# An earlier release of a conversion's exponent tile, and GpSimd subtractions made in two halves, in a fused attention and gated-layer kernel

## The chip, the cores and the metric

The kernel runs on one core of one Trainium2 chip. A core has TensorE (matrix products; in the rows PE, its weight loads PEld), VectorE (DVE), ScalarE (ACT), GpSimd (POOL) and SyncE (SP, which here issues most DMAs). Each works through its own list of instructions in order and waits on semaphores for the others. The metric is the device time of one execution in microseconds; lower is better.

## The reference

Two layers, one behind the other, in float32. The first is an attention in which a query sees only the keys of its own hash bucket (4 batches, 8 heads, 768 positions, 64 columns a head); the second is a gated layer on 3072 rows of 512 columns, with 1536 columns between.

```python
q_bits = np.einsum('bhsd,dk->bhsk', q, proj) > 0      # 6 sign bits, k likewise
mask = q_bucket[:, :, :, None] == k_bucket[:, :, None, :]
scores = np.where(mask, q @ k.T / 8, -1e9)
attn = softmax(scores) @ v                             # 4 x 8 x 768 x 64
x = attn as 3072 x 512
gate = 1 / (1 + np.exp(-(x @ w_gate)))                 # weights are float64
out = (gate * (x @ w_val)) @ w_out
```

The three weights of the gated layer arrive as float64 and the chip's engines calculate in float32.

## The kernel before, in words

**Two stages.** Stage 1 is the attention, with the first two products of the gated layer at its end, and beside it the conversion of most weights. Stage 2, from 428.7 us of the span, is the gated layer: TensorE goes through products `z` (L1178) and `y` (L932) with weights that GpSimd's queue fetches back (L1728).

**The attention.** Work goes in pairs of heads (16 pairs, named batch_pair, as 3_1), each in two groups of three tiles of 128 query rows. For a tile and head, a *score task* of TensorE (8 matmuls, `sc`, L1551 and L1557) fills one of three PSUM places called `two`; VectorE takes the least value and moves the tile to SBUF (`e<-sc`, L1569), which frees the place; ScalarE forms the exponentials (L1578). When the six exponentials of a group are there, six *turns* (12 transposes each, `tp<-ident,e`, L1614) go through the same three places `two`; each is copied back by ScalarE or VectorE (`e<-tp`, L1620). Then come six *value tasks* (`pv`, L1630), which add up in another place of PSUM, and the division `xs` (L1637).

Ahead of a pair, its k and q are turned (`tk`, `tq`, L1358), copied (`rawk`, `rawq`), rounded to a high part (`kh`, `qh`, ScalarE or GpSimd), and the low part is the rest, `kl = rawk - kh` (L1389, GpSimd or VectorE, 768 columns). The parts of q are also sent through DMAs to swapped halves (`qsl`, `qsh`, L1418). The *hash* of a pair (`h`, L1452) gives sign bits on VectorE (`kq<-h`, L1458), which are sent to DRAM (`bd<-kq`, L1461) and back in another layout (`kq<-bd`, L1468 and L1470); the first score task of the pair needs them.

**A weight conversion** (`floats`, L674) makes float32 out of 512 columns of float64. VectorE picks the exponent bits (`exponent`, L689, tile `ex`), ScalarE shifts them (L692), VectorE picks the mantissa (`mantissa`, L697, tile `mf`), adds the low word (L702) and puts the sign in `ex` (L707); GpSimd multiplies `mf` by `ex` (`scaled`, L712). In `load_pair` (L802) four sums (L821 to L824) make seven blocks out of four, and the result is split in a high part (L830) and a low part (L833, 896 columns), which are sent to DRAM (L836) for stage 2. 34 conversions stand in stage 1: 20 for the pairs, and 10 of `w_out` and 4 for the early products, which have no sums and are split in L766 and L769. 6 more stand in stage 2, where VectorE and ScalarE do GpSimd's part.

**What sets the order.** A planner (`Plan.order`) goes through a model of the engines and writes each engine's instructions in the order in which they start in it. Every task names what it needs (`after`), which counted places it takes and gives back (`take`, `give`), and a key. TensorE's order is a written table, `ORDER`; the other engines take the ready task with the smallest key, and the table `SHIFT` moves keys. `stock` holds the number of places; `mid1=1` is the one place that a conversion of stage 1 takes ahead of its exponent and gives back after its low part. Since the conversions' tasks are numbered in both tables, each new task gives new tables.

Of the kernel before, what the change touches and what calls it, by code (L numbers as in the profile page):

```python
# [111 lines left out]
]  # L112
SHIFT = {
# [394 lines left out]
def lsh_attention_glu_kernel(ctx, tc, q, k, v, proj, w_gate, w_val, w_out, out):  # L508
# [132 lines left out]
    def busy():  # L641
        nc.tensor.matmul(idle, zero[:, :P], zero, start=True, stop=True)  # L642

    W_KEY, W_STEP, W_MORE = 2.0, 1.5, 0.2
    stock = dict(
        one=2, two=3, moe=1, y=0, kr=1, qr=1, vr=2, h=2, e=3, st=3, su=3, sv=2, rb=2, xs=3,
        raw1=1, mid1=1, raw2=2, mid2=1, wk=1, xr=1, x2=1, x3=1, ob=3,
        t=0, zt=0, ws0=0, ws1=0, ws2=0, xb=0, r0=0, r1=0, r2=0, x1=0, x4=0, x5=0, x6=0, wk2=0,
    )
    WS = 3  # L650
# [1126 lines left out]
```

## Time and profile before

| | |
|---|---|
| median of 3 runs | 964.09 us (963.86 to 966.96) |
| the profiled execution's own time | 965.6 us |
| its span | 963.8 us |
| TensorE busy | 952.0 us (99%) |
| VectorE, ScalarE, GpSimd busy | 608.2, 548.2, 274.3 us |
| stage 1 (to 428.7 us) / stage 2 | 428.7 us / 535.1 us of the span |

The span is the time from the first to the last instruction in the profile; 1.8 us of the execution's own time lie around it. "Busy" of TensorE counts a matmul from its start to a modelled end, so small waits between matmuls hide in it; starts of one kind of task, one behind the other, show them better.

### The profile page before, as it was taken

Reading aid. Unit: us, or ns where it says so; the run is one execution under the profiler, and the core shown is the slowest. Engines: PE = TensorE matmul, PEld = TensorE weight load, DVE = VectorE, ACT = ScalarE, POOL = GpSimd, SP = SyncE. Lnnn points to the kernel's source line nnn. Section 1 sums busy time; section 2 is a strip of 40 time slices with the busy share of each in tenths; the row PEclk is TensorE's granted clock in tenths of the full one; section 3 lists DMA queues with packets and bytes.
Section 4 is the critical chain, followed back from the end, with each engine's and each line's share of the span. In section 5 each row is a group of like instructions: output and inputs, shape, how many; then the busy total and the mean of one; then the engine's idle time right before and its main releaser. Section 6 shows DMA issues by size and latency. Waiting matters only on the chain.

```text
span 963.8 us, 20105 instructions
## 1 busy us (share of the span) xinstructions
PE 952.0 (99%) x8067; PEld 774.8 (80%) x8070; DVE 608.2 (63%) x1173; ACT 548.2 (57%) x993; POOL 274.3 (28%) x325
## 2 busy tenths in 40 slices
PE   9999999999999999999999999999999999999998
PEld 5666665666666567689999999999999999999997
DVE  7999898999899898676656743334633336333332
ACT  5988898898888889554334433324433235333322
POOL 4444655666765665630000000000000000000000
PEclk9999999999999999999999999999999999999999
DMA  7666888888897877489966774444744444644421
GB/s 186 175 194 189 224 252 241 244 249 238 263 268 213 233 228 228 171 315 411 370 237 230 280 262 175 153 153 154 271 170 158 170 177 173 222 154 153 154 78 66
DMA packets 116606, 204.37 MB, mean 212 GB/s; under 512 B 63456, under 2 KB 87968, under 8 KB 110624
## 3 DMA queue, kind: packets, MB, share of 16 engines
q1 hardware_dynamic: 107456, 118.08, 39.9%
q0 software_dynamic: 6688, 84.42, 23.7%
q8 instruction: 63, 1.03, 0.4%
q10 hardware_dynamic: 2368, 0.59, 0.3%
q14 instruction: 31, 0.25, 0.1%
HBM read 147.84 MB, written 43.42 MB: 198 GB/s over the span
## 4 chain that ended last, share of the span: by engine, by line
PE 92%; DVE 4%; DMA 2%; ACT 1%; issue 1%; SPq 0%; ACTq 0%; DVEq 0%
PE y L932 20%; PE pv L1630 12%; PE zBg L1178 10%; PE zBv L1178 10%; PE sc L1557 9%; PE tp L1614 7%; PE zDv L1178 5%; PE zDg L1178 5%; PE sc L1551 4%; PE zAg L1178 2%; PE zAv L1178 2%; PE h L1452 1%; DVE e L1569 1%; PE zg L896 1%; PE zv L896 1%; PE idle L642 1%
## 5 line engine op out<-in xcount | busy, mean ns | idle before, releaser
L1569 DVE TENSOR_SCALAR_CACHE_REDUCE e<-sc 128x768 f32<-128x768 f32 x192 | 177.1, 952 | 20.3 <-PE sc L1557 18.5
L1578 ACT ACTIVATE e<-e,st 128x768 f32<-128x768 f32 x192 | 178.9, 933 | 15.1 <-DVE e L1569 13.2
L932 PE MATMUL y<-wo,gh 128*128 128x512 f32 x480 | 151.0, 396 | 0.0
L1630 PE MATMUL pv<-e,vr 128*64 128x384 f32 x768 | 140.7, 496 | 0.0
L1620 ACT COPY e<-tp 128x768 f32<-128x768 f32 x144 | 112.2, 795 | 27.9 <-PE tp L1614 27.1
L1614 PEld LDWEIGHTS tp<-ident,e 64*128 64x128 f32 x2304 | 87.0, 138 | 45.7 <-issue 13.7
L1178 PE MATMUL zBg<-x,wsg 128*128 128x384 f32 x552 | 111.0, 335 | 0.0
L1178 PE MATMUL zBv<-x,wsv 128*128 128x384 f32 x552 | 110.7, 335 | 0.0
L1178 PEld LDWEIGHTS zBg<-x,wsg 128*128 128x128 f32 x552 | 98.2, 188 | 6.6 <-ACT t1g L1186 0.4
L1178 PEld LDWEIGHTS zBv<-x,wsv 128*128 128x128 f32 x552 | 98.3, 188 | 6.0
L932 PEld LDWEIGHTS y<-wo,gh 128*128 128x128 f32 x480 | 89.9, 187 | 15.2
L1614 PE MATMUL tp<-ident,e 64*128 64x64 f32 x2304 | 99.6, 226 | 1.8 <-DVE e L1569 0.9
L1271 ACT CAST gh<-zt 128x384 fp32r<-128x384 f32 x92 | 47.1, 514 | 95.1 <-DVE zt L1266 75.5
L932 PE MATMUL y<-wo,gl 128*128 128x512 f32 x240 | 93.2, 388 | 0.0
L1557 PE MATMUL sc<-kh,ql 64*128 64x384 f32 x192 | 89.8, 468 | 0.0
L1557 PE MATMUL sc<-kh,qsl 64*128 64x384 f32 x192 | 89.8, 468 | 0.0
L1630 PEld LDWEIGHTS pv<-e,vr 128*64 128x64 f32 x768 | 48.2, 136 | 51.3 <-issue 43.0
L1728 POOL DMA_DIRECT2D wsv<-kzv x23 | 12.2, 532 | 236.9 <-PE zDg L1178 224.6
L1728 POOL DMA_DIRECT2D wsg<-kzg x23 | 12.3, 536 | 227.4 <-PE zDv L1178 206.9
L1250 ACT ACTIVATE sig<-sig 128x384 f32<-128x384 f32 x69 | 36.2, 525 | 61.7 <-DVE sig L1193 61.6
L1274 DVE TENSOR_TENSOR gl<-zt,gh 128x384 fp32r<-128x384 f32 x92 | 51.0, 554 | 29.2 <-ACT gh L1271 29.2
L1551 PE MATMUL sc<-kq 64*128 64x384 bf16 x384 | 64.8, 328 | 2.3 <-ACT e L1620 1.1
(214 smaller groups left out, 1964.4 us busy)
## 6 DMA issues: line engine op xcount, KB each, us to landing
wsg<-kzg POOLq DMA_DIRECT2D x23, 1792.0 KB, 8.1
wsv<-kzv POOLq DMA_DIRECT2D x23, 1792.0 KB, 7.6
kzg<-wkg SPq DMA_DIRECT2D x12, 896.0 KB
kzv<-wkv SPq DMA_DIRECT2D x12, 896.0 KB
rawg<-in_moe_w_gate_dram SPq DMA_DIRECT2D x14, 512.0 KB
rawv<-in_moe_w_val_dram SPq DMA_DIRECT2D x14, 512.0 KB
vr<-in_v_dram SPq DMA_DIRECT2D x16, 384.0 KB
rb<-rd SPq DMA_DIRECT2D x64, 96.0 KB
```

Source lines behind the costliest of these rows:

```text
L932: nc.tensor.matmul(acc, a[:, slot, ts_], w, start=(first and i == 0), stop=(last and i == 2), skip_group_check=cols != slice(None),)
L1178: nc.tensor.matmul(acc, streams[n, jp][:, c, wa, a_], X[x_][:, xa, c], start=first and c == 0 and i == 0, stop=c == 1 and i == 2, skip_gro ...
L1250: lambda blk=blk: nc.scalar.activation(sig[:, blk], w["B"][:, :GN] if blk == 2 else sig[:, blk], AF.Sigmoid),
L1271: nc.scalar.copy(side["h"][:, blk], w["z", blk])
L1274: eng.tensor_sub(side["l"][:, blk], w["z", blk], f(side["h"][:, blk]))
L1551: nc.tensor.matmul(sc[:, j, :GN], kq[z["h"]][rows, 2 + 2 * g + h, t * P : (t + 1) * P], kq[z["h"]][rows, h], start=True, stop=False, tile_ ...
L1557: nc.tensor.matmul(sc[:, j, :GN], q_[rows, c], z["k" + x][rows, h * GN : (h + 1) * GN], start=False, stop=(m == 2), tile_position=(j * D, 0),)
L1569: nc.vector.tensor_scalar(sp(e), gz["sc", t, h][:, :, :GN], -MASKED * SCALE, None, op0=ALU.min, op1=ALU.min, accum_out=gz["st", t][:, h : ...
L1578: nc.scalar.activation(e, e, AF.Exp, bias=st[:, h : h + 1], scale=-1.0, accum_out=gz["su"][:, h * GT + t : h * GT + t + 1],)
L1614: nc.tensor.transpose(tp[:, r, at_ : at_ + D], gz["e", t, h][rows, c * P : (c + 1) * P], ident[rows, rows], tile_position=(r * D, 0),)
L1620: copy(gz["e"][:, :, c * P : (c + 1) * P].rearrange("p n (r d) -> p r n d", r=2), gz["tp", c][:, :, :GN].rearrange("p r (n d) -> p r n d", ...
L1630: nc.tensor.matmul(gz["pv"][rows, :GN], z["v"][:, h, c], gz["e"][:, h * GT : (h + 1) * GT, c * P : (c + 1) * P], start=(c == 0), stop=(c = ...
```

## The change

The exponent tile has a place of its own, `ex1`, taken by `exponent` and given back when GpSimd's `scaled` is done with it; `mid1` is now taken by `mantissa`. The low part of a converted pair in stage 1 is made in two pieces of 512 and 384 columns, and the low parts of k and q in two pieces of 384, and each piece may go to GpSimd or VectorE. Both tables of the order are new throughout.

```diff
     stock = dict(
-        raw1=1, mid1=1, raw2=2, mid2=1, wk=1, xr=1, x2=1, x3=1, ob=3,
+        raw1=1, mid1=1, ex1=1, raw2=2, mid2=1, ex2=1, wk=1, xr=1, x2=1, x3=1, ob=3,
...
-        b1 = add(key, "dve", 336, exponent, after=[a], take=["mid" + own], port=0.92)
+        b1 = add(key, "dve", 336, exponent, after=[a], take=["ex" + own], port=0.92)
         b2 = add(key, "act", 628, shifted, after=[b1])
-        c1 = add(key, "dve", 400, mantissa, after=[b1], port=0.92)
+        c1 = add(key, "dve", 400, mantissa, after=[b1], take=["mid" + own], port=0.92)
...
-            key, "dve" if last else "pool", 680 if last else 1240, lambda: scaled(nc.vector if last else nc.gpsimd), after=[d], port=0.92
+            key, "dve" if last else "pool", 680 if last else 1240, lambda: scaled(nc.vector if last else nc.gpsimd), after=[d], give=["ex" + own], port=0.92
...
-        def low(eng):
-            eng.tensor_sub(y["w"][:, 1], y["f"], f(y["w"])[:, 0])
+        def low(eng, c=slice(None)):
+            eng.tensor_sub(y["w"][:, 1, c], y["f"][:, c], f(y["w"])[:, 0, c])
...
-        m = add(key, [("dve", 1005, lambda: low(nc.vector))] if last else
-                [("pool", 2078, lambda: low(nc.gpsimd)), ("dve", 1005, lambda: low(nc.vector))], after=[h], give=["mid" + own], port=0.92)
+        m = h
+        for cut, n_ in ((slice(0, 4), 4), (slice(4, SL), SL - 4)) if not last else ((slice(None), SL),):
+            m = add(key, [("dve", 1005, lambda: low(nc.vector))] if last else
+                    [("pool", 180 + 280 * n_, lambda cut=cut: low(nc.gpsimd, cut)), ("dve", 70 + 134 * n_, lambda cut=cut: low(nc.vector, cut))],
+                    after=[h, m], give=["mid" + own] if last or n_ < 4 else [], port=0.92)
...
-                eng.tensor_sub(z[n + "l"], z["raw", n], f(z[n + "h"]))
+                c = slice(half * GN, (half + 1) * GN)
+                eng.tensor_sub(z[n + "l"][:, c], z["raw", n][:, c], f(z[n + "h"][:, c]))
...
-                needs.append(add(
-                    n_, [("pool", 1930, lambda n=n: part(n, "l", nc.gpsimd)), ("dve", 870, lambda n=n: part(n, "l", nc.vector))],
-                    after=[a], port=0.92,
-                ))
+                b_ = None
+                for half in range(2):
+                    b_ = add(
+                        n_, [("pool", 1030, lambda n=n, half=half: part(n, "l", nc.gpsimd, half)),
+                             ("dve", 470, lambda n=n, half=half: part(n, "l", nc.vector, half))],
+                        after=[a, b_], port=0.92,
+                    )
+                needs.append(b_)
```

What the new order does to the lists of instructions is shown at three places. First GpSimd where pair 2_3's k and q are split (`kl`, `ql`) beside a conversion's split (`wk`). Before:

```order
L1389 TENSOR_TENSOR kl2_3_4831<-rawk2_3_4797,kh2_3_4830 128x768
L830 CAST wkg31_4883<-mfg3_1_4735 128x896
L833 TENSOR_TENSOR wkg31_4883<-mfg3_1_4735,wkg31_4883 128x896
L1389 TENSOR_TENSOR ql2_3_4897<-rawq2_3_4871,qh2_3_4896 128x768
L1585 TENSOR_SCALAR su2_148<-su2_148 128x6
```

And now:

```order
L1422 TENSOR_TENSOR kl2_3_4862<-rawk2_3_4822,kh2_3_4861 128x384
L859 CAST wkv31_4890<-mfv3_1_4749 128x896
L862 TENSOR_TENSOR wkv31_4890<-mfv3_1_4749,wkv31_4890 128x512
L862 TENSOR_TENSOR wkv31_4890<-mfv3_1_4749,wkv31_4890 128x384
L1422 TENSOR_TENSOR ql2_3_4959<-rawq2_3_4929,qh2_3_4958 128x384 x2
```

Each subtraction stands as two; the other half of `kl` has moved to VectorE. Over the whole kernel GpSimd's 25 subtractions of 768 columns become 45 of 384, and VectorE's 5 become 15; of the 20 of 896 columns, 35 pieces stay on GpSimd and 5 go to VectorE.

Second VectorE, around one conversion (`exo`, `mfo`) between the least values of score tasks (`e<-sc`). Before:

```order
L1569 TENSOR_SCALAR e2_1_0_4315,st2_1_0_0_4314<-sc2_1_0_0_1_4317 128x768
L689 TENSOR_SCALAR exo5_4369<-rawo5_4184 128x512
L1620 COPY e2_0_1_4084<-tp2_0_1_0_4336 128x2x6x64
L697 TENSOR_SCALAR mfo5_4380<-rawo5_4184 128x512
L702 SCALAR_TENSOR_TENSOR mfo5_4380<-rawo5_4184,mfo5_4380 128x512
L707 SCALAR_TENSOR_TENSOR exo5_4369<-rawo5_4184,exo5_4369 128x512
```

And now, at a conversion close by:

```order
L718 TENSOR_SCALAR exo4_4112<-rawo4_3981 128x512
L1606 TENSOR_SCALAR e2_0_1_4100,st2_0_1_0_4099<-sc2_0_1_0_1_4090 128x768
L1606 TENSOR_SCALAR e2_0_1_4100,st2_0_1_1_4138<-sc2_0_1_1_0_4103 128x768
L726 TENSOR_SCALAR mfo4_4145<-rawo4_3981 128x512
L1626 RECIPROCAL su1_147<-su1_147 128x6
L1628 STREAM_TRANSPOSE sv2_0_0_4150<-su1_147 128x32
L731 SCALAR_TENSOR_TENSOR mfo4_4145<-rawo4_3981,mfo4_4145 128x512
L736 SCALAR_TENSOR_TENSOR exo4_4112<-rawo4_3981,exo4_4112 128x512
```

The exponent now stands two least values ahead of the mantissa here; over the 34 conversions of stage 1 it stands 1 to 4 places ahead in both orders.

Third TensorE at the end of the scores of pair 1_1, where the turns of its first group begin. Before:

```order
L1557 MATMUL sc1_1_1_2_1_2829<-kh1_1_2062,qh1_1_2117 128x384
L1614 MATMUL tp1_1_0_2_2841<-ident_170,e1_1_0_2505 128x64 x12
L1630 MATMUL pv1_1_0_2855<-e1_1_0_2505,vr1_1_2458 64x384 x2
L1630 MATMUL pv1_0_1_2564<-e1_0_1_2237,vr1_0_1950 64x384 x2
L1630 MATMUL pv1_1_0_2855<-e1_1_0_2505,vr1_1_2458 64x384 x2
L1630 MATMUL pv1_0_1_2564<-e1_0_1_2237,vr1_0_1950 64x384 x4
L1614 MATMUL tp1_1_0_3_2883<-ident_170,e1_1_0_2505 128x64 x12
```

And now:

```order
L1594 MATMUL sc1_1_1_2_1_2873<-kh1_1_2078,qh1_1_2130 128x384
L1651 MATMUL tp1_1_0_2_2888<-ident_170,e1_1_0_2466 128x64 x12
L1651 MATMUL tp1_1_0_3_2902<-ident_170,e1_1_0_2466 128x64 x12
L1588 LDWEIGHTS kq0_208
L1588 MATMUL sc1_2_0_0_0_2917<-kq0_208 128x384
```

A score task, two turns and a score task now follow each other with no value task between. Such a group (score task, two turns, another user of `two`) stands in stage 1 once before and four times now. TensorE's instructions are the same in number and kind, and apart from the first products of stage 2 they stand in the same order there.

## Rows read from the trace of the kernel before

**Rows 1.** View of stretches: from:to, length, busy PE, PEld, DVE, ACT, POOL; clock; DMA.

```profile
0.00:428.70 428.70, 420.73 (x5286) 280.94 (x5290) 374.68 (x752) 352.52 (x618) 250.06 (x281) 1.00 0.77 226
428.70:960.00 531.30, 531.26 (x2782) 493.82 (x2780) 233.07 (x421) 195.29 (x375) 24.24 (x45) 1.00 0.54 201
```

**Rows 2.** Timeline from 104.5 us: start, length, instruction [idle before, releaser].

```profile
105.12 1.41 DVE L689 TENSOR_SCALAR exg<-rawg 128x512 int32<-128x512 int32 x1
106.18 1.02 POOL L1387 CAST qh<-rawq 128x768 fp32r<-128x768 f32 x1
...
107.29 1.83 POOL L1389 TENSOR_TENSOR ql<-rawq,qh 128x768 fp32r<-128x768 f32 x1
107.31 2.09 DVE L697 TENSOR_SCALAR mfg<-rawg 128x512 int32<-128x512 int32 x1
...
112.99 0.34 PE L1551 MATMUL sc<-kq 64*128 64x384 bf16 x2 [0.91 <-ACT e L1620]
```

**Rows 3.** Timeline from 157.5 us.

```profile
159.42 2.07 DVE L697 TENSOR_SCALAR mfv<-rawv 128x512 int32<-128x512 int32 x1
...
162.01 0.52 PE L1452 MATMUL h<-rawk,w_all 128*32 128x384 f32 x2 [1.05 <-DVE xs L1637]
```

**Rows 4.** Timeline from 324 us.

```profile
325.93 2.06 DVE L697 TENSOR_SCALAR mfv<-rawv 128x512 int32<-128x512 int32 x1
...
331.59 0.59 PE L1614 MATMUL tp<-ident,e 64*128 64x64 f32 x12 [0.67 <-ACT e L1620]
```

**Rows 5.** Timeline from 124.5 us.

```profile
127.63 1.28 POOL L712 TENSOR_TENSOR mfv<-mfv,exv 128x512 f32<-128x512 f32 x1
...
127.84 1.48 DVE L870 TENSOR_TENSOR xl<-xr,xh 128x384 fp32r<-128x384 f32 x1
...
130.26 0.59 PE L1614 MATMUL tp<-ident,e 64*128 64x64 f32 x12 [0.93 <-DVE e L1569]
```

**Rows 6.** Instructions on one tile (rawg): ns min/median/max, first and last start.

```profile
L697 DVE TENSOR_SCALAR mfg<-rawg x12: 387/420/2092, 28.4 to 398.9; 128x512 int32<-128x512 int32 x12
```

**Rows 7.** Groups of stage 1: xcount | busy, mean ns | idle before.

```profile
L1620 DVE COPY e<-tp 128x768 f32<-128x768 f32 x48 | 45.3, 951 | 5.2 <-PE tp L1614 5.1
L870 DVE TENSOR_TENSOR xl<-xr,xh 128x384 fp32r<-128x384 f32 x5 | 4.8, 979 | 0.4 <-POOL xh L867 0.4
L1620 ACT COPY e<-tp 128x768 f32<-128x768 f32 x144 | 112.2, 795 | 27.9 <-PE tp L1614 27.1
L689 DVE TENSOR_SCALAR exg<-rawg 128x512 int32<-128x512 int32 x12 | 6.9, 575 | 0.0
L920 POOL TENSOR_TENSOR gl<-gf,gh 128x384 fp32r<-128x384 f32 x2 | 2.1, 1032 | 12.0 <-ACT gh L919 12.0
```

**Rows 8.** The page's group of such a subtraction on VectorE in stage 2.

```profile
L1274 DVE TENSOR_TENSOR gl<-zt,gh 128x384 fp32r<-128x384 f32 x92 | 51.0, 554 | 29.2 <-ACT gh L1271 29.2
```

**Rows 9.** Timeline of TensorE from 272 us: score task, two turns, score task.

```profile
273.55 0.33 PE L1551 MATMUL sc<-kq 64*128 64x384 bf16 x2
...
275.46 0.34 PE L1551 MATMUL sc<-kq 64*128 64x384 bf16 x2
```

**Rows 10.** Timeline of TensorE from 264 us: value tasks, score task, turn, score task.

```profile
265.72 0.87 PE L1630 MATMUL pv<-e,vr 128*64 128x384 f32 x4
266.52 0.34 PE L1551 MATMUL sc<-kq 64*128 64x384 bf16 x2
...
267.22 0.54 PE L1614 MATMUL tp<-ident,e 64*128 64x64 f32 x12
267.58 0.34 PE L1551 MATMUL sc<-kq 64*128 64x384 bf16 x2
```

**Rows 11.** Timeline from 308 us: hash, bits on their way, first score task.

```profile
309.36 0.52 PE L1452 MATMUL h<-rawk,w_all 128*32 128x384 f32 x2
...
317.84 0.93 SPq L1470 DMA_DIRECT2D kq<-bd  x2
...
322.41 0.71 PE L1551 MATMUL sc<-kq 64*128 64x384 bf16 x2 [0.23 <-DMA kq<-bd]
```

More of the change, by code (lines that the diff above doesn't have):

```diff
@@ L1378, in raw, with part @@
                 eng.tensor_scalar(o, i_, -SCALE, None, op0=ALU.mult)
-        def part(n, x, eng):
+        def part(n, x, eng, half=0):
             if x == "h":
```

587 rows, old and new, of tables (ORDER, SHIFT) are left out of this document.

## The prediction

> **What bounds the kernel now.** I read first the table of engines and the windows of the two stages. In stage 2 TensorE is busy for all of its 531.30 us but 0.04 [rows 1], and the change leaves its list there as it was, apart from the first products. So only the end of stage 1, 428.7 us, can move. There TensorE is busy 420.7 us, VectorE 374.7, ScalarE 352.5, GpSimd 250.1: the other three have 54, 76 and 178 us of idle time, and TensorE waits seldom. I then listed TensorE's idle times and followed each back on the timeline. The four long ones have one cause. Three times VectorE's mantissa op, 2.06 to 2.09 us instead of its median 0.42 [rows 2 to 4, 6], runs beside a GpSimd subtraction of 768 columns that began just before it: `ql` starts at 107.29 and lasts 1.83, the mantissa starts at 107.31 and ends at 109.40. Some 1.65 us are lost on VectorE, the least values and copies behind it are late, and TensorE stands still for 0.91, 1.05 and 0.67 us. The fourth time VectorE's own subtraction `xl` of two SBUF inputs, 1.48 instead of its mean 0.98, meets GpSimd's `scaled` (1.28), and TensorE waits 0.93 [rows 5, 7]. The clock was at its full level, 2.4 GHz (1.00), throughout [rows 1], so it gives nothing.
>
> **The change part by part.**
>
> *Halves of the k and q subtractions.* The row nearest to a half is GpSimd's subtraction of 384 columns, 1.03 us [rows 7]. A mantissa that meets one waits at most that, instead of 1.65. If VectorE gets its turn between two halves, the three idles can go, and with them 0.91 + 1.05 + 0.67 = 2.63 us. Bounds: 0 (the mantissa waits out both halves, or another wait fills the gap) and -2.63. I take **-2.6**, since even the worst case leaves VectorE 0.6 us earlier than now and most meetings would be shorter. Two halves of 1.03 last 0.2 us longer than one whole of 1.83; 45 pieces cost GpSimd some 5 us, which 178 us of idle time hide. Without that cover it would make the low parts late, and so the swapped halves of q.
>
> *Where `xl` goes.* The new order gives VectorE one of the eight `xl`, where it had five. I take the 0.93 as gone: **-0.9** (bounds 0 and -0.93).
>
> *Loads.* Counted from the lists, VectorE loses ten turn copies at 0.951 and four `xl` at 0.979 [rows 7]: -13.4. It gains five halves' worth of columns of k and q (15 of 384 for 5 of 768) and five pieces of weights' low parts, each between 0.55 [rows 8] and 0.98 (as `xl`, beside GpSimd), and the four sums of one pair at up to 0.55 each: +5.5 to +12.0. So -7.9 to -1.4; I take -4.5. ScalarE gains the ten copies at 0.795 [rows 7] and gives up four roundings of about that size: +4.8. How much of an engine's time reaches TensorE? At the four places VectorE lost 1.67 + 1.65 + 1.64 + 0.50 = 5.5 us and TensorE 3.6, but elsewhere VectorE's slow ops cost nothing that I could find. I take a third of VectorE's and, as ScalarE has more idle time, a sixth of its: -1.5 + 0.8 = **-0.7** (bounds: -4.0, if half of 7.9 reaches it and nothing of ScalarE's, and +1.1, if a third of 1.4 is gained and a third of 4.8 lost).
>
> *The new order.* A score task, two turns and a score task without a value task between stand once before, at 273.55, and the second score comes 1.91 us later [rows 9]; with value tasks ahead, score to turn and turn to score are 0.70 and 0.36, and a second turn would add the 0.36, 1.42 in all [rows 10]. So a group costs 0.49, as the copy that frees a place of `two` is waited for. Three more: 0 to 1.5, taken as **+0.7**, for copies may be done sooner. At pair 3_1 two turns now stand straight ahead of a value task, which needs the second turn's copy: 0.54 for the turn and 0.80 for the copy against 0.85 of other work, 0 to 0.6, **+0.3**.
>
> *The exponents.* They may now stand while the conversion before still has its mantissa place, so they can meet GpSimd's work oftener. An exponent takes 0.575 in the mean [rows 7], against the 0.42 of an undisturbed pick [rows 6]; if all 34 lost as much again, VectorE would be 5.3 us longer, of which a third is 1.8. Both orders have them one to four places ahead of their mantissa, so I take **+0.3** (0 to 1.8).
>
> Sum: -2.6 - 0.9 - 0.7 + 0.7 + 0.3 + 0.3 = **-2.9**. The profiled execution's own time is 965.6, which gives 962.7. The median of the three runs is 1.5 below it: **961.1 us**, 0.3% under 964.09. About 0.3% (2.9 us) is what a measurement of this kernel can tell from no change, so the forecast lies on that bound. With all terms at their better ends it would be -2.6 - 0.9 - 4.0 = -7.5, or 956.6.
>
> **The rivals.**
>
> *The new order takes it back.* Groups at 1.5, the value task at 0.6, exponents at 1.8: -2.6 - 0.9 - 0.7 + 3.9 = -0.3, 963.8. For it: the places `two` bind in rows 9. Against: the planner chose the groups where copies are early in its model.
>
> *Halving does nothing.* GpSimd's second half follows the first at once, and VectorE waits for both. Then -2.6 goes: 963.7. For it: both engines are ready then, and nothing in the lists parts the halves. Against: behind the `kl` ahead of 105 us it was VectorE's exponent that ended its long wait first (1.41 us from 105.12), and GpSimd's rounding `qh` took 1.02 [rows 2].
>
> *Two-input halves on VectorE.* VectorE has twenty two-input pieces now, and if each lasts as `xl` (0.98) instead of some 0.65, that is 6.6 us, of which a third, 2.2, reaches TensorE: 963.3. For it: the 1.48 beside `scaled` [rows 5]. Against: `xl`'s mean already holds such a meeting.
> The Trainium skill, "SBUF — State Buffer", section "Who interferes with whom", says why such pieces might wait: a VectorE instruction with two SBUF inputs contends with a GpSimd instruction that reads SBUF, for a pair of ports that one of them holds for its whole instruction. By that rule the mantissa of rows 2 would start its own 0.42 at 107.29 + 1.83 = 109.12 and end at 109.54; the row ends at 109.40, so the trace nearly agrees, and halves would shorten the wait as forecast while the moved subtractions join the contention.
>
> *Slower: the sign bits come late.* From the hash at 309.36 to the first score at 322.41 took 13.05 us, of which TensorE waited 0.23 for `kq<-bd` [rows 11]: the bits' chain is 13.0 us. I counted TensorE's work between hash and first score in both orders by the durations of rows 10. Pair 0_3 now has 10.0 us where it had 16.7, pair 0_2 11.3 (14.9), 1_2 11.8, 0_1 12.0, 2_3 12.3 (14.4), 3_0 12.4 (15.5). At a chain of 13.0 these lack 3.0 + 1.7 + 1.2 + 1.0 + 0.7 + 0.6 = 8.2 us, and the time would be 961.1 + 8.2 = 969.3. SyncE issues the bits' four loads behind other transfers (`qsh`, `qsl`, a conversion's store), whose waits spread them. It decides from a chain of about 12.8: there the shortfalls are 7.0 us, past the 5.8 that part 961.1 from the slower bound of 967.0; at 12.0 they are 2.9, which ends where it began. Against: rows 11 are the one place where the trace shows this wait, and its order was made with the chain known.
>
> **How the numbers follow.** Forecast 0.50, of which 0.40 lies past the bound, since the bounds of its terms reach further down (own range 956.5 to 962.5); order takes it back 0.14; halving does nothing 0.08; two-input halves 0.08; late bits 0.20, most of it slower. So faster 0.40, same 0.41, slower 0.19. The range holds the forecast, the three rivals on the side of no change and about half of the late bits: 956.5 to 968.0.
>
> **What would show it.** Right: no mantissa op above 1.5 us in stage 1; the idles of 0.91, 1.05 and 0.67 gone from TensorE's list and none above 0.5 in their place; stage 2 beginning at about 425.8; stage 2 as long as before. The order's cost shows as 1.9 us from score to score over two turns. Halving fails if mantissas still take 2 us beside two halves. The sign bits show as TensorE idle that ends on `kq<-bd`, first at pair 0_3. Wrong otherwise: an idle that ends on a conversion's weights at the stages' seam, or more of VectorE's time reaching TensorE than a third.

## The result and the profile after

The changed kernel takes 972.23 us (median of six runs, 969.56 to 976.06) against 963.9 for the kernel before: a ratio of 1.0081, 95% interval 1.0068 to 1.0094. It is slower by 0.8%, some 7.8 us, where 0.3% faster was forecast, and lies above the range. The profiled execution is the quickest of the six; its span is 967.8 us, against 963.8, so the two traces show 4.0 of the 7.8 us. Stage 2 begins at 431.7 us, against 428.7 before and 425.8 in the forecast.

The stretches of the profile after, to be held against [rows 1] (from:to, length, busy PE, PEld, DVE, ACT, POOL; clock; DMA):

```profile
0.00:428.70 428.70, 417.93 (x5269) 278.77 (x5270) 371.21 (x755) 352.94 (x621) 254.34 (x318) 1.00 0.76 224
428.70:960.00 531.30, 530.81 (x2781) 494.14 (x2780) 234.67 (x423) 195.32 (x375) 25.71 (x46) 1.00 0.55 201
```

In the first 428.7 us VectorE works 3.5 us less, as meant, and yet TensorE does 2.8 us less work: it waits. Whom it waits for, up to 440 us (line, releaser: total, times, longest):

```profile
PE sc L1588 <- DMA kq<-bd: 2.6, 3, 1.6
PE zg L928 <- ACT ob L1006: 1.6, 1, 1.6
PE sc L1588 <- DVE e L1606: 1.5, 6, 0.4
...
PE zo L964 <- DVE gl L952: 1.0, 1, 1.0
...
PE zBg L1210 <- ACT t16g L1218: 0.5, 1, 0.5
```

The waits of rows 2 to 5 are gone. Two new ones lead: the sign bits (`kq<-bd`, 2.6 us where the kernel before shows 0.23 [rows 11]) and `zg <- ACT ob`, at the seam between the stages, where the kernel before shows none. The mantissa ops, in the view of one line (ns min/median/max), to be held against [rows 6]:

```profile
L726 DVE TENSOR_SCALAR mfg<-rawg x12: 385/430/1057, 27.2 to 387.6; 128x512 int32<-128x512 int32 x12
L726 DVE TENSOR_SCALAR mfv<-rawv x12: 414/422/1223, 37.1 to 396.8; 128x512 int32<-128x512 int32 x12
```

None lasts longer than 1.22 us, where one took 2.09. So the halves do let VectorE in sooner.

The first `zg` of the seam and the first `y` of stage 2, before and now:

```profile
405.32 0.44 PE L896 MATMUL zg<-xh,we 128*128 128x384 f32 x1
449.45 0.39 PE L932 MATMUL y<-wo,gl 128*128 128x512 f32 x1
```

```profile
406.88 0.44 PE L928 MATMUL zg<-xh,we 128*128 128x384 f32 x1
453.38 0.39 PE L964 MATMUL y<-wo,gl 128*128 128x512 f32 x1
```

So TensorE comes to the seam 1.6 us later and loses 2.4 us more in it (46.5 us against 44.1); from there on the two traces run alike. The longest wait of the seam, on the timeline of the changed kernel (start, length, instruction [idle before, releaser]):

```profile
421.53 0.55 POOL L1765 DMA_DIRECT2D wsv<-kzv  x1
421.68 2.27 DVE L1093 TENSOR_TENSOR T<-xb,B 128x768 f32<-128x768 f32 x1
422.10 1.02 POOL L902 TENSOR_TENSOR xl<-xr,xh 128x384 fp32r<-128x384 f32 x1
423.98 0.83 ACT L1067 CAST x<-T 128x768 fp32r<-128x768 f32 x1 [3.31 <-DVE T L1093]
424.72 0.59 ACT L1006 ACTIVATE ob<-zo 128x512 f32<-128x512 f32 x1
425.36 0.44 PE L928 MATMUL zg<-xh,we 128*128 128x384 f32 x1 [1.57 <-ACT ob L1006]
```

It is read from the bottom. `zg` needs the PSUM place that `ob` empties. The product that `ob` copies was done at about 422.5, but `ob` stands behind the cast `x<-T`, which waits for VectorE's `T`. `T` takes 2.27 us; in the kernel before the same subtraction takes 0.96:

```profile
421.75 0.96 DVE L1061 TENSOR_TENSOR T<-xb,B 128x768 f32<-128x768 f32 x1
```

It spans GpSimd's fetch `wsv` and the low part `xl`, which the new order moved from VectorE to GpSimd. A fetch alone does not lengthen such an op: in stage 2 of the same trace `gl<-zt,gh`, which reads two SBUF tensors too, begins inside a fetch 19 times and takes its usual 0.55 us each time, as here:

```profile
451.75 0.53 POOL L1765 DMA_DIRECT2D wsg<-kzg  x1 [8.84 <-PE zDv L1210]
451.95 0.55 DVE L1306 TENSOR_TENSOR gl<-zt,gh 128x384 fp32r<-128x384 f32 x1
```

So the rows point at `xl`. But `T` starts 0.42 us ahead of it, and no run puts this `xl` back on VectorE: that it is what holds `T` is argued and not shown.

### The profile page after: what moved, and what is told of

Read it like the earlier page. It is cut to its first block, busy times and chain, and to the rows that moved or that the text cites. A ratio compares the mean times of both kernels' runs of the same rounds, so it can differ in the third digit from the quotient of the medians.

```text
span 967.8 us, 20183 instructions
## 1 busy us (share of the span) xinstructions
PE 952.7 (98%) x8070; PEld 776.2 (80%) x8070; DVE 606.3 (63%) x1178; ACT 550.2 (57%) x999; POOL 280.0 (29%) x364
## 4 chain that ended last, share of the span: by engine, by line
PE 84%; DVE 6%; DMA 4%; ACT 2%; POOL 2%; issue 1%; SPq 1%; DVEq 0%; ACTq 0%; POOLq 0%
PE y L964 20%; PE zBv L1210 10%; PE pv L1667 10%; PE zBg L1210 10%; PE sc L1594 7%; PE tp L1651 6%; PE zDv L1210 5%; PE zDg L1210 5%; PE sc L1588 3%; DVE e L1606 3%; PE zAv L1210 2%; PE zAg L1210 2%; DMA kq<-bd 2%; DMA bd<-kq 1%; PE idle L671 1%
## 5 line engine op out<-in xcount | busy, mean ns | idle before, releaser
L1657 ACT COPY e<-tp 128x768 f32<-128x768 f32 x154 | 119.8, 794 | 21.7 <-PE tp L1651 20.9
```

Of the source, the lines that this page charges most:

```text
L1657: copy(gz["e"][:, :, c * P : (c + 1) * P].rearrange("p n (r d) -> p r n d", r=2), gz["tp", c][:, :, :GN].rearrange("p r (n d) -> p r n d", ...
```

## The experiments

Each ratio is against runs of the kernel before on the same chip; 0.001 is 0.96 us.

**The changed kernel once more**, unaltered, for a second trace.

> The changed kernel once more, unaltered, for a second trace. Of its six timed runs the shown one took 969.6 us at a mean clock of 1.000, four others 972.2 to 976.1 at 0.996 to 0.998. If a fall of TensorE's clock adds the difference, a trace of a run near 972 to 974 shows a stretch of some 8 us at half clock, and the idle time ahead of it names the cause: the sign bits (theory A: an idle of TensorE that ends on the transfer kq<-bd) or the seam of the stages near 425 us (theory B).

It took 973.14 us, and its trace has a fall of TensorE's clock. The stretches around the seam, which lies 2.1 us later here (the clock is the number ahead of the last two):

```profile
426.00:428.00 2.00, 0.58 (x3) 0.58 (x4) 1.83 (x3) 1.96 (x4) 0.00 (x0) 1.00 0.94 394
428.00:430.00 2.00, 2.00 (x9) 2.00 (x7) 1.73 (x2) 1.20 (x3) 0.00 (x0) 0.50 1.02 437
430.00:432.00 2.00, 2.00 (x9) 2.00 (x9) 1.15 (x2) 0.74 (x2) 0.00 (x0) 0.65 0.99 420
432.00:434.00 2.00, 2.00 (x14) 2.00 (x13) 0.53 (x2) 0.47 (x1) 0.00 (x0) 1.00 1.02 432
```

TensorE worked 0.58 of 2 us, behind a wait of 1.57, and then had half of its clock (0.50, 1.2 GHz) for all of one stretch and most of the next: 1.0 + 0.7 = 1.7 us at the most, not the 4 expected. From the first `zg` to the first `y` it takes 1.6 us longer than in the first trace (48.1 against 46.5). The other 2 us of the 3.6 by which this span exceeds the first were lost before the seam. There the bits' waits add up to 2.9 (with a new one at pair 3_1, 323.13) instead of 2.6; with other new waits, of scores and turns, the list explains about half of the 2 us. So theory B names the place of the fall; theory A was still open.

**Free sign bits**, in the changed kernel and in the kernel before: all scores read the first pair's bits, and the masks by the other pairs' own bits are left out.

```diff
-  kq[z["h"]][rows, 2 + 2 * g + h, ...], kq[z["h"]][rows, h], ...   # scores
+  kq[0][rows, 2 + 2 * g + h, ...], kq[0][rows, h], ...
...
-  to = kq[z["h"]][j * D : j * D + QB]                              # loads of later pairs
+  to = kq[1][j * D : j * D + QB]
```

> The changed kernel, but all pairs' scores read the sign bits of the first pair, so that no score waits for its own pair's bits; the hash, its bits and their transfers are all still made. Output is not the reference's. Theory A (late sign bits, with the fall of the clock behind them, are the loss): 965 to 967 us, 5 to 7 below the changed kernel's 972.2, clock 1.000 in all runs. Theory B (the seam): only the 2.6 us of waits on kq<-bd go, 969 to 970, and clocks of 0.996 to 0.998 stay.

> The kernel before with the same edit. Its waits on kq<-bd add up to some 0.2 us, so both theories expect 963.5 to 964.2, no change. If it gets faster by more than 2 us, the bits cost the kernel before too, in a way that its idle times did not show.

Changed: 966.85 us, ratio 1.0031 (1.0020 to 1.0042). Before: 963.88, ratio 1.0002 (0.9993 to 1.0012). Late bits cost the new order some 0.0050, 4.8 us of 7.8, and the old one nothing that this can tell. That is nearly twice the waits that a trace shows for them (2.6 and 2.9). The clock differs too: its mean over a timed run was 1.000, 1.000, 0.997, 0.996, 0.996 and 0.998 in the six runs of the changed kernel, and 0.999 or 1.000 in all six with free bits, although their trace still has the wait of 1.57 at the seam.

**Halves in the old order.** Each GpSimd subtraction is issued as two, back to back, with all else in its place.

```diff
-  eng.tensor_sub(z[n + "l"], z["raw", n], f(z[n + "h"]))
+  for c in (slice(0, GN), slice(GN, S)) if eng is nc.gpsimd else (slice(None),):
+      eng.tensor_sub(z[n + "l"][:, c], z["raw", n][:, c], f(z[n + "h"][:, c]))
```

> The kernel before in its old order, with every GpSimd subtraction of stage 1 (k, q and the weights' low parts) issued as two, one right behind the other; nothing else is moved. If VectorE gets its turn between the halves: no mantissa op above 1.5 us in stage 1, the idles of 0.91, 1.05 and 0.67 us of TensorE gone or halved, 961.3 to 962.5 us. If the second half follows before VectorE gets its turn (the rival 'halving does nothing'): mantissas of 2 us stay, 963.5 to 965.

963.36 us, ratio 0.9990 (0.9980 to 1.0000): some 1 us, not the 2.6 of the forecast, and hardly apart from no change. The longest mantissas, in the view of one line:

```profile
L697 DVE TENSOR_SCALAR mfg<-rawg x12: 384/418/436, 27.4 to 396.9; 128x512 int32<-128x512 int32 x12
L697 DVE TENSOR_SCALAR mfv<-rawv x12: 384/420/1257, 49.6 to 387.1; 128x512 int32<-128x512 int32 x12
```

the longest of them, beside two halves:

```profile
159.31 2.15 POOL L1391 TENSOR_TENSOR ql<-rawq,qh 128x384 fp32r<-128x384 f32 x2
159.34 1.26 DVE L697 TENSOR_SCALAR mfv<-rawv 128x512 int32<-128x512 int32 x1
```

and two of TensorE's rows:

```profile
128.87 0.58 PE L1616 MATMUL tp<-ident,e 64*128 64x64 f32 x12 [1.55 <-DVE e L1571]
...
152.99 0.33 PE L1553 MATMUL sc<-kq 64*128 64x384 bf16 x1 [0.97 <-DMA kq<-bd]
```

So VectorE does get its turn between two halves that follow at once, and of the three idles two are gone, while the one of 1.05 is down to 0.23. But what was behind them takes their place: a least value behind an `xl` that waits for GpSimd's `xh` at 128.87 (0.93 before, 1.55 now), and pair 1_2's bits. Nor is the first of the three idles in every execution of the old order. The run above of the kernel before with free bits took 963.47 us in its profiled execution, its subtractions are whole, and it has at the place of [rows 2]:

```profile
107.42 2.11 POOL L1389 TENSOR_TENSOR ql<-rawq,qh 128x768 fp32r<-128x768 f32 x1
107.44 0.40 DVE L697 TENSOR_SCALAR mfg<-rawg 128x512 int32<-128x512 int32 x1
```

The two start 0.02 us apart as in [rows 2], but here it is GpSimd that takes longer, by 0.3 us, and the idle of 0.91 is not there.

**The seam.** In the emitted list of the changed kernel, one task of ScalarE goes ahead of another:

```diff
  ACT
-   CAST x5_0<-T2_0
    ACTIVATE ob2_0_0<-zo2_0_0
+   CAST x5_0<-T2_0
```

> The changed kernel with one swap on ScalarE at the seam of the stages: the third copy ob<-zo, which frees a PSUM place that TensorE waits for, stands ahead of the cast x5<-T, which waits for VectorE; nothing else moves. If the seam's 1.57 us wait (ACT ob) and the fall of the clock behind it are a loss of their own: the wait goes, the clock stays at 1.000, and the time falls by 1.6 to 3.5 us, to 968.5 to 970.6. If another wait takes its place (the next user of that PSUM place, or the cast): 971.5 to 973.

968.13 us, ratio 1.0037 (1.0023 to 1.0051), 4.2 us better than the changed kernel. ScalarE's row, where the wait of 1.57 is gone:

```profile
421.89 0.60 ACT L1009 ACTIVATE ob<-zo 128x512 f32<-128x512 f32 x1 [1.85 <-PE zo L967]
423.37 0.84 ACT L1070 CAST x<-T 128x768 fp32r<-128x768 f32 x1 [0.89 <-DVE T L1096]
```

Not all of the 1.57 is won: two later waits at the seam, `zv <- sig` (0.34) and `zBg <- t16g` (0.49, there before the swap too), leave 45.4 us from the first `zg` to the first `y`, 1.2 less than without the swap. With a fall like the one above (1.6) that makes 2.8 of the 4.2. In seven of the nine timed runs the mean clock is 0.999 or 1.000, in the other two 0.996 and 0.998.

**Both.** The swap and free bits together.

> The swap at the seam together with the first pair's sign bits for all pairs (output is not the reference's). If late bits and the seam are the whole loss and add up, 966.85 (free bits alone) less 1.6 to 2.4: 964.4 to 965.3, so that at most 1.5 us over the kernel before are left to the rest of the order. If the seam's wait only moves: 966 to 967.

965.80 us, ratio 1.0013 (1.0003 to 1.0023). Alone they gave 4.8 and 4.2 us, together 6.6: they overlap, and 1.3 us are left. The seam takes 45.3 us here, against 44.1 in the kernel before: most of the 1.3 is still lost there.

**Whole subtractions in the new order.** On top of the run before, all halves are undone; then those of the weights alone. The whole subtraction stands at the first half's place and on its engine, so some work changes its engine as well: VectorE has ten whole subtractions of k and q where it had fifteen halves, and none of the weights.

```diff
-  c = slice(half * GN, (half + 1) * GN)
-  eng.tensor_sub(z[n + "l"][:, c], z["raw", n][:, c], f(z[n + "h"][:, c]))
+  if half == 0:
+      eng.tensor_sub(z[n + "l"], z["raw", n], f(z[n + "h"]))
...
-  [("pool", 180 + 280 * n_, lambda cut=cut: low(nc.gpsimd, cut)), ...
+  [("pool", 180 + 280 * n_, lambda n_=n_: low(nc.gpsimd) if n_ == 4 else None), ...
```

> As the run with the swap and free bits, but each two halves are one whole subtraction again, at the first half's place and on its engine (20 of k and q on GpSimd, 10 on VectorE; all 20 of the weights on GpSimd). If the halves save TensorE what the forecast said, mantissas beside whole subtractions take 2 us again and the time is 1.5 to 3 us above that run, 966 to 968. If halving does nothing for the time: within 0.7 of it.

> As the run with swap and free bits (965.80), but the 20 low parts of the weights are whole on GpSimd (896 columns) and only k and q stay in halves. The forecast counted the halves of k and q alone. If they carry it: 965.5 to 967.0. If the whole weights' subtractions of 2.1 us are what the new order can't bear (973.60 with everything whole): 970 to 973.5.

All whole: 973.60 us, ratio 1.0099 (1.0075 to 1.0123). Only the weights whole: 969.04, ratio 1.0041 (1.0029 to 1.0054). Both theories of the first run missed, and both of the second: undoing the weights' halves costs 2.7 us, undoing those of k and q another 5.6. In this order undoing the halves costs 8.3 us, not 1.5 to 3; what the change of engine and place has in that is not parted from it. Mantissas take up to 2.05 us again, and not they alone; the next op of a conversion, which adds the low word and reads two SBUF inputs, with halves and whole:

```profile
L734 DVE SCALAR_TENSOR_TENSOR mfo<-rawo,mfo x10: 649/691/1553, 60.3 to 359.2; 128x512 f32<-128x512 uint32 x10
```

```profile
L734 DVE SCALAR_TENSOR_TENSOR mfo<-rawo,mfo x10: 648/691/2344, 60.5 to 363.5; 128x512 f32<-128x512 uint32 x10
```

**The early release alone**, in the kernel before.

```diff
-  raw1=1, mid1=1, ...                       exponent: take=["mid" + own]
+  raw1=1, mid1=1, ex1=1, ...                exponent: take=["ex" + own], mantissa: take=["mid" + own], scaled: give=["ex" + own]
```

> The kernel before with only the early release of the exponent tile: TensorE's table and the shifts of keys are the old ones, subtractions stay whole, and the other engines' lists follow from the planner. The forecast's term is +0.3 (0 to 1.8): 963.8 to 965.6. If earlier exponents meet GpSimd's whole subtractions more often, exponents of 1 to 2 us are seen more often than now and it is at the upper end; if the release gives VectorE better places, 962 to 963.5.

1008.02 us, ratio 1.0443 (1.0405 to 1.0481), far from both. TensorE's longest wait is 10.3 us, of `zBg` on ScalarE's `x`; the mantissas of one tile, in the view of one line:

```profile
L697 DVE TENSOR_SCALAR mfg<-rawg x12: 402/420/725, 28.1 to 432.8; 128x512 int32<-128x512 int32 x12
```

Of these mantissas none is above 0.73 us, but the last starts at 432.8 instead of 398.9 [rows 6]. The clock falls to half twice, behind TensorE's waits near 432 and 452 us. A place is the planner's bookkeeping: with it the other engines' lists are made anew, while TensorE's table and the shifts stay those of another program, and the conversions fall behind. This run prices a table that doesn't fit, not an exponent.

**SyncE's order.** The changed kernel with the swap at the seam, and the bits' transfers ahead: at pair 1_1, then at all pairs.

```diff
  SP, pair 1_1
-   DMA qsl_1<-ql_1
    DMA bd<-kq
+   DMA qsl_1<-ql_1
...
-   DMA kzg<-wkg
    DMA kq<-bd
+   DMA kzg<-wkg
```

> The changed kernel with the swap at the seam, and at pair 1_1 alone two swaps in SyncE's list: the store bd<-kq ahead of the loads qsl<-ql, and the second load kq<-bd ahead of the store kzg<-wkg. In three traces of the new order TensorE waits longest there for kq<-bd, 1.4 to 1.8 us near 125. If SyncE's order at that pair is the cause: that wait goes, 966.3 to 967.0, some 1.2 to 1.8 below the 968.13 of the seam's swap alone. If the bits are late there because TensorE has too little work between hash and first score: the wait stays, 968 to 968.5.

> The same at all 15 pairs: the store bd<-kq stands directly behind what makes the bits, and the two loads kq<-bd directly behind one another; with the swap at the seam. If late issues on SyncE are the loss: 965.8 to 966.5, as with free bits (965.80). If what SyncE then issues later (the swapped halves, the divisors) is waited for instead: 967.5 to 969.

At one pair: 967.56 us, ratio 1.0028 (1.0017 to 1.0040), which the intervals don't part from the seam's swap alone (1.0037); it lies between the two forecasts. At all: 966.36, ratio 1.0015 (1.0006 to 1.0024). First SyncE at pair 1_1 in the changed kernel, whose first score waits 1.62:

```profile
113.43 1.35 SPq L1451 DMA_DIRECT2D qsl<-ql  x2
114.88 0.54 SPq L1494 DMA_DIRECT2D bd<-kq  x1
...
118.20 0.93 SPq L1501 DMA_DIRECT2D kq<-bd  x2
119.24 0.36 SPq L865 DMA_DIRECT2D kzg<-wkg  x1
119.65 1.35 SPq L1503 DMA_DIRECT2D kq<-bd  x2
...
125.94 0.50 PE L1588 MATMUL sc<-kq 64*128 64x384 bf16 x2 [1.62 <-DMA kq<-bd]
```

and with the two swaps there, where that wait is gone and the one left for bits is at pair 2_1:

```profile
113.93 0.39 SPq L1497 DMA_DIRECT2D bd<-kq  x1
114.38 1.11 SPq L1454 DMA_DIRECT2D qsl<-ql  x2
...
119.33 0.90 SPq L1506 DMA_DIRECT2D kq<-bd  x2
...
224.72 0.54 PE L1591 MATMUL sc<-kq 64*128 64x384 bf16 x2 [1.17 <-DMA kq<-bd]
```

With all pairs done so no wait on `kq<-bd` is left in the trace, and the time is that of free bits within the intervals. So SyncE's order made the bits late, with TensorE's order as it was, and it can be put right without leaving anything out.

**The old order with halves and a later `xl`.** The last `xl` of the first early product goes behind a least value.

```diff
  DVE
-   xl0_0<-xr0_0,xh0_0
    e1_1_0<-sc1_1_0_0_0
    su<-su
    sv<-su
+   xl0_0<-xr0_0,xh0_0
```

> The kernel before with back-to-back halves, and one more swap: the last xl of the first early product on VectorE stands behind a least value (e<-sc) instead of ahead of it; in the trace of halves alone TensorE waits 1.55 us there (127.32 to 128.87). If that wait is what the halves' gain went into: 961.8 to 962.6, the fastest so far. If the wait only moves: 963 to 963.6 as with halves alone (963.36).

963.36 us, ratio 0.9988 (0.9975 to 1.0000): as halves alone. The wait of 1.55 shrank to 1.14, for the `xl` ahead of it, beside GpSimd's (1.44), still makes VectorE late:

```profile
126.45 1.44 POOL L874 TENSOR_TENSOR xl<-xr,xh 128x384 fp32r<-128x384 f32 x1
...
126.95 1.35 DVE L874 TENSOR_TENSOR xl<-xr,xh 128x384 fp32r<-128x384 f32 x1
...
129.70 0.59 PE L1619 MATMUL tp<-ident,e 64*128 64x64 f32 x12 [1.14 <-DVE e L1574]
```

No version measured here is faster than the kernel before by more than these two, 0.1%, and both intervals reach no change.

## Why the prediction was wrong

**"Apart from the first products", and no term for them.** This step failed first: the sum puts the seam at nothing. I took it as the same work in another order. There the new order gives GpSimd an `xl`, VectorE's `T` lasts 2.27 us beside it, and ScalarE's list passes the delay on to TensorE: 1.57 us, 2.4 with the later waits of the seam, and in the second trace 1.6 more by half clock. One swap takes back 4.2 us. The seam could be seen to be tight: "the four long ones" leaves out the wait `zo <- gl` of 1.0 us at 416 us, longer than three of the four, which is in both kernels.

**No term for the sign bits in the sum; "late bits 0.20".** The forecast itself puts late bits at nothing; they cost 4.8 us, of which the traces show 2.6 to 2.9 as waits. The rival names this wait, and names SyncE's order among what spreads it, but it reckons with one chain of 13.0 us and with TensorE's work between hash and first score alone. Of its six pairs one waited: 0_3, for 0.61 us where 3.0 were said. The longest wait, 1.62, was at pair 1_1, which is not on the list: 15.6 us lie between its hash (110.31) and its score, and SyncE issued its bits behind `qsl`. With SyncE's list put right the waits went, at TensorE's old work. That the rival's 969.3 came near is luck.

**"-2.6" for the halves.** The mechanism was right: no mantissa above 1.26 us in the old order with halves or 1.25 in the new, and the rival that halving leaves the mantissas at 2 us is refuted. The size was wrong: in the old order some -1.0 us. I added three idles as if nothing stood behind them, but the next waits took their place, at 128.87 and 152.99. And I read them from an execution that was 1.5 us above the median, though the first of them is not in the second trace of the old order, and then took off the 1.5 as well: in part the same time was counted twice. (962.7 less 1.5 is 961.2, too, not 961.1.) In the new order, which needs them, undoing the halves costs 8.3 us.

The mantissa reads one SBUF tensor. The sentence on two SBUF inputs, by which the prediction works out an end at 109.54, does not speak of it; that it waits beside a GpSimd subtraction is shown by the rows alone.

**"-0.9" for `xl`.** The wait of [rows 5] is gone, but the piece moved to GpSimd is part of the seam's loss, as far as the rows above show it.

**"+0.7" and "+0.3" for the new order.** The price of a group was right by luck: what stands between the scores of [rows 9] is a turn of k and one of q (`tk`, `tq`), not two turns of exponentials. At three groups in the trace after, score to score takes 1.92, 2.06 and 1.93 us (from 149.09, 263.92 and 360.23), 0.5 to 0.6 above the 1.42, as the sign said. So three cost some 1.6 us, the upper bound and not 0.7. The value task behind two turns waits 0.52, within its 0 to 0.6:

```profile
358.73 1.57 PE L1667 MATMUL pv<-e,vr 128*64 128x384 f32 x8 [0.52 <-ACT e L1657]
...
360.23 0.34 PE L1588 MATMUL sc<-kq 64*128 64x384 bf16 x2
...
362.16 0.34 PE L1588 MATMUL sc<-kq 64*128 64x384 bf16 x2 [0.32 <-DVE e L1606]
```

**"+0.3" for the exponents.** The 34 exponents of stage 1 take VectorE 17.2 us in the trace after, where they took 19.5, and the longest 1.28 us instead of 2.08. So the term had the wrong sign; what it is worth to TensorE is not parted from the rest.

**"-0.7" for loads** isn't seen apart. VectorE is 3.5 us less busy, near what was said (4.5), but with bits and seam's swap put right the order is still 1.3 us slower than the old one, where -2.9 was forecast. By the traces 1.2 us of that stand at the seam. The attention gains nothing either, and one reason is that GpSimd's work still holds VectorE up at other places. With all bits ahead, the longest of TensorE's waits in the attention comes about so:

```profile
320.68 2.44 POOL L865 TENSOR_TENSOR wkg<-mfg,wkg 128x512 fp32r<-128x512 f32 x2
...
323.47 0.19 DVE L1629 RECIPROCAL su<-su 128x6 f32<-128x6 f32 x1 [1.21 <-POOL su L1625]
...
324.41 2.46 POOL L1425 TENSOR_TENSOR kl<-rawk,kh 128x384 fp32r<-128x384 f32 x2
...
324.64 1.38 DVE L734 SCALAR_TENSOR_TENSOR mfv<-rawv,mfv 128x512 f32<-128x512 uint32 x1
...
326.95 0.34 PE L1591 MATMUL sc<-kq 64*128 64x384 bf16 x2 [1.14 <-DVE e L1609]
```

VectorE first stands idle for 1.21 us, for GpSimd's `su` behind two halves of `wkg`. Then an op that adds the low word meets the two halves of `kl` and takes 1.38 instead of its median 0.69. Both make the least value late that TensorE waits for. The Trainium skill, "SBUF — State Buffer", section "Who interferes with whom", says that a VectorE instruction with two SBUF inputs contends with a GpSimd instruction that reads SBUF; the rows of that op agree. I had weighed that rule for the subtractions that move to VectorE, and not for the two-input ops of the 34 conversions.

The times of the seam's swap and of free bits overlap by 2.4 us. Falls of the clock that need both the late bits and the seam's wait would do that, and the mean clocks of the timed runs go with it: most of the falls are gone with either change alone. But only one trace of this order shows where a fall lies, and why bits that come late 100 us and more before the seam should bring it on is not shown.

## What to carry to other kernels

When an order is made anew, read every engine's list at the joins of stages and every queue's list ahead of a long transfer chain, and not only the engine that bounds: the two largest losses here were one instruction standing behind another that waited, on ScalarE and on SyncE. Idle times that follow on one another don't add up to a gain; ask what is late next, and whether a second trace of the same kernel has them too. Price a cut with the order that will be run: halves were worth some 1 us in the order made without them, and undoing them cost 8 in the order made with them. A planner's table belongs to the program that it was made for: here one place more, with the old table, cost 4%.

## What the hardware showed that was not expected

Two GpSimd halves issued back to back still let a waiting VectorE mantissa in: at most 1.26 us instead of 2.09. Which of the two waits is not settled by the lists: with starts 0.02 us apart, the mantissa took 2.09 and `ql` 1.83 in one execution, 0.40 and 2.11 in another. A GpSimd DMA issue alone left a VectorE subtraction of two SBUF tensors at its 0.55 us, 19 times of 19. TensorE's clock fell to half for some 3.4 us behind a wait of 1.57 us in one trace and not in another with the same wait (967.8 us span, clock 1.00 throughout the seam).
